# The remainder's low-part passes of two outputs of each first-layer weight pair as two 64-row matmuls in two halves of the TensorE array

## The chip, the core and the metric

The kernel is one program on one core of a Trainium2 chip. The metric is the device time of one execution in microseconds (us), median of several runs. The core has a matrix engine (TensorE, PE in the profile, with its weight loads listed apart as PEld), a vector engine (DVE), a scalar engine (ACT), GpSimd (POOL) and a queue that issues the transfers (SP). They run side by side and wait for each other through semaphores.

## What is computed

The input x has 2048 tokens of width 576. It is normalised per token, and a sum of three terms is returned: x itself, a local attention on the normalised x, and a two-layer network with the mish activation on it:

```python
def _B_ref(x, w1, b1, w2):
    h = jnp.einsum("bsd,df->bsf", x, w1) + b1          # 576 -> 4608
    sp = jnp.log1p(jnp.exp(-jnp.abs(h))) + jnp.where(h > 0, h, jnp.zeros_like(h))
    act = h * jnp.tanh(sp)
    return jnp.einsum("bsf,fd->bsd", act, w2)           # 4608 -> 576

x = A_x
xn = _layernorm(x, axis=-1)
return x + _A_ref(xn, A_wqkv, A_wo) + _B_ref(xn, B_w1, B_b1, B_w2)
```

The change is in the first layer of that network, x times w1.

## The kernel before

**Numbers in two parts.** A float32 operand is split into a high part (a cast to the matmul's own format) and a low part (what the cast dropped). A product is then three matmuls: high by high, low by high, high by low. `prod` (L652) issues these three for two blocks of 128 contraction rows, six matmuls of 128x512.

**The contraction of 576** is four blocks of 128 rows and a remainder of 64. The remainder is not run as 64 rows: the last 64 rows of every weight are there twice, one copy below the other, so a remainder weight has 128 rows. On the x side the 128 rows hold the high part in one half and the low part in the other. One matmul with the high weights then gives high by high and low by high at once. A second one, with the low weights, adds high by low; only the half with the high part of x matters there, and the other half adds low by low, which is far below the precision that is kept. `rest` (L661) issues the two: `wl` 0 with the high weights, `wl` 1 with the low ones. The second is the half-filled pass of the title.

**The x tiles.** A half `hf` of the tokens has two blocks `b` of 512 tokens. `XTs[hf, b]` (tile `xt`) holds x transposed: slots 0 to 3 the high blocks, slot 4 the remainder, 5 to 8 the low blocks. For b = 1 a slot 9 holds the remainder of the difference of the two token blocks. `transpose_split` (L68) fills it, once for each 128 tokens: five or six transposes on PE, a copy to the high slots on ACT, a subtraction for the low slots on DVE. For the remainder the ACT copy writes all 128 rows, and the DVE subtraction (L89) replaces rows 64 to 127 by the low part, for slot 4 and, where it exists, slot 9 in one instruction.

**The first layer** runs over 18 pairs `q` of 128-column weight blocks for each half `hf`, 36 in all. With a Strassen-like scheme of seven products a pair gives four outputs (two token blocks by two weight blocks). `m1_part` (L715) issues it in six parts. Banks of PSUM accumulate: `cur[1]` (tile `h1`), `cur[2]` (`h2`), `cur[3]` (`h3`). Snapshots of `cur[1]` are copied out by ACT in `take` (L691: c11, c21, c22), and `mish` (L694) adds a bank to a snapshot on DVE (L702), applies the activation on ACT (L703) and, in the first half, splits the result. Parts 0, 3, 4 and 5 each end with a `rest`: on `cur[2]`, `cur[1]`, `cur[3]` and `cur[1]`. Parts 4 and 5 are the two that the change touches: part 4 finishes `cur[3]` with the weight `wa` and slot 4, part 5 finishes `cur[1]` with the weight `wc` and slot 9.

**The order** is written out by hand. `quad` puts the parts of a pair in a plan, between chunks of the second layer (`m2_pair` L747, `p_item`, `m2_cols` L858: 24 matmuls of 128x288 each). In 34 of the 36 pairs part 4 comes ahead of part 5, with a chunk of the second layer between them in nearly all of them; in the first pair of each half part 5 comes ahead. Attention (POOL products, DVE sums), weight splitting and transfers are placed by the same plan, so that each engine has one fixed sequence.

Of the kernel before, what the change touches and what calls it, by code (L numbers as in the profile page):

```python
# [8 lines left out]
F32 = mybir.dt.float32  # L9
# [8 lines left out]
P = 128  # L18
# [21 lines left out]
def block_kernel(ctx: ExitStack, tc: tile.TileContext, x, wq, wo, w1, b1, w2, mask, out):  # L40
    nc = tc.nc
# [27 lines left out]
    def transpose_split(src, dst, col, extra=None, pair=False):  # L69
        n = next(tpn)  # L70
        if pair:
            ta, tb = (ps.tile([P, 512], F32, tag="out", bufs=4, name=f"tt{k}_{n}") for k in range(2))
        else:
            ta = ps.tile([P, 512], F32, tag="h", bufs=4, name=f"ta_{n}")
            tb = ps.tile([P, 512], F32, tag="h", bufs=4, name=f"tb_{n}")
        for k in range(KT):
            nc.tensor.transpose(ta[:, k * P:(k + 1) * P], src[:, k * P:(k + 1) * P], ident)
        nc.tensor.transpose(tb[:, 0:P], src[:, KT * P:(KT + 1) * P], ident)
        if extra is not None:
            nc.tensor.transpose(tb[:, P:2 * P], extra, ident)  # L80
        tav = ta.rearrange("p (k t) -> p k t", k=KT)
        hi = dst[:, 0:KT, col:col + P]
        nc.scalar.copy(hi, tav)  # L83
        nc.vector.tensor_sub(dst[:, 5:5 + KT, col:col + P], tav, hi.bitcast(F32))
        e = 1 if extra is None else 2
        hr = dst[:, KT:KT + 5 * e - 4:5, col:col + P]
        tbv = tb.rearrange("p (k t) -> p k t", k=KT)[:, 0:e]
        nc.scalar.copy(hr, tbv)
        nc.vector.tensor_sub(hr[64:P], tbv[64:P], hr[64:P].bitcast(F32))  # L89

    XTs = {}
    rems = {}
# [93 lines left out]
    def ln_transpose(hf, b, jj):  # L186
        if jj == 0:
            XTs[hf, b] = sb.tile([P, 9 + b, TB], F32R, tag=f"xt{b}", bufs=1, name=f"xt_{hf}_{b}")
        xn = xns[hf, b * JB + jj]
        if (b, jj) == (0, 0):  # L190
            rems[hf] = sb.tile([P, JB, P], F32, tag="tt", bufs=2, name=f"rem_{hf}")
        rem = rems[hf][:, jj, :]
        if b == 0:
            nc.gpsimd.tensor_copy(rem, xn[:, KT * P:])
        else:
            nc.gpsimd.tensor_tensor(out=rem, in0=rem, in1=xn[:, KT * P:], op=ALU.subtract)
        transpose_split(xn, XTs[hf, b], jj * P, rem if b else None, (hf, b) == (1, 0) and jj < 3)
# [449 lines left out]
    cur = {}  # L647
    late = []

    def bank(hf, q, n):  # L650
        cur[n] = ps.tile([P, TB], F32, tag="h", bufs=4, name=f"h{n}_{hf}_{q}")
        return cur[n]  # L652

    def prod(ph, wt, off, X, hi, lo, first, last):
        seq = [(off + k, wl, xs + k) for k in range(2) for wl, xs in ((0, hi), (0, lo), (1, hi))]
        for i, (wk, wl, xs) in enumerate(seq):
            nc.tensor.matmul(ph, wt[:, wl, wk * P:(wk + 1) * P], X[:, xs, :],  # L657
                             start=first and i == 0, stop=last and i == len(seq) - 1,
                             skip_group_check=True)

    def rest(ph, wt, off, X, xs):  # L661
        for wl in range(2):
            nc.tensor.matmul(ph, wt[:, wl, off * P:(off + 1) * P], X[:, xs, :], start=False, stop=wl == 1,  # L663
                             skip_group_check=True)

    seven = lambda hf, q: hf == 1 and q <= 2 * OC
# [19 lines left out]
    def take(hf, q, name):  # L686
        if seven(hf, q):
            t = cur[name] = raw_act(q, *dict(c11=(0, 0), c21=(1, 0), c22=(1, 1))[name])
        else:
            t = cur[name] = sb.tile([P, TB], F32, tag="mn", bufs=5, name=f"{name}_{hf}_{q}")  # L690
        nc.scalar.copy(t, cur[1])  # L691

    def mish(hf, q, b, j, ph, t=None):
        f = 2 * (Q1[q] if hf else q) + j  # L694
        n = f"{hf}_{b}_{f}"
        fresh = t is None
        if fresh:
            t = raw_act(q, b, j) if seven(hf, q) else sb.tile([P, TB], F32, tag="mn", bufs=5, name=f"mn_{n}")

        def run():  # L700
            if not fresh:
                nc.vector.tensor_tensor(out=t, in0=ph, in1=t, op=ALU.add)  # L702
            nc.scalar.activation(t, ph if fresh else t, AF.Mish, bias=b1c[:, f:f + 1])  # L703
            if seven(hf, q):
                held_[q, f"A{b + 1}{j + 1}"] = f"A{b + 1}{j + 1}"
                return
            a = acts[hf, q, b, j] = sb.tile([P, 2, TB], F32R, tag=f"a{b}", bufs=(3, 2)[b], name=f"act_{n}")
            nc.scalar.copy(a[:, 0, :], t)  # L708
            nc.gpsimd.tensor_tensor(out=a[:, 1, :], in0=t, in1=a[:, 0, :].bitcast(F32), op=ALU.subtract)  # L709
        if q or b != j:  # L710
            pend.append(run)
        else:
            late.append(run)

    def m1_part(hf, q, part):  # L715
        X0, X1 = XTs[hf, 0], XTs[hf, 1]
        if part == 5 and late:
            for fn in late[::-1]:
                fn()
            late.clear()  # L720
        wa, wc, t0, t1 = (done.get((k, hf, q)) for k in ("wa", "wc", "t0", "t1"))
        if part == 0:
            prod(bank(hf, q, 1), wa, 0, X0, 0, 5, True, True)
            take(hf, q, "c11")
            prod(bank(hf, q, 2), wa, 2, X0, 2, 7, True, False)
            rest(cur[2], wa, 4, X0, 4)
            mish(hf, q, 0, 0, cur[2], cur["c11"])
        elif part == 1:
            prod(bank(hf, q, 3), t1, 0, X1, 0, 5, True, True)
        elif part == 2:  # L730
            prod(cur[1], t0, 2, Ss[hf, 1], 0, 2, False, True)
            take(hf, q, "c21")
        elif part == 3:
            prod(cur[1], t0, 0, Ss[hf, 0], 0, 2, False, False)
            rest(cur[1], wc, 2, X1, 4)
            take(hf, q, "c22")
        elif part == 4:
            prod(cur[3], t1, 2, X1, 2, 7, False, False)
            rest(cur[3], wa, 4, X1, 4)
            mish(hf, q, 1, 0, cur[3], cur["c21"])  # L740
        else:
            prod(cur[1], wc, 0, Ss[hf, 2], 0, 2, False, False)
            rest(cur[1], wc, 2, X1, 9)
            mish(hf, q, 0, 1, cur[1])
        if part == 3:
            mish(hf, q, 1, 1, cur[3], cur["c22"])
# [406 lines left out]
    def mi(hf, q, part, alias=None):  # L1153
        add(("m", hf, q, part), lambda: m1_part(hf, q, part), alias=alias)
# [178 lines left out]
    def spot(hf, q, i):  # L1333
        return at["s", hf, q, i]
# [97 lines left out]
    for n in range(8):  # L1432
        c, k = divmod(n, 4)
# [57 lines left out]
    k = marks[0] - 1  # L1491
    for n in range(2 * steps):
        t = n * total / (2 * steps)
        if n == steps:
            k = max(k, spot(1, 0, 0) + 1)
        k = next(k for k in range(k + 1, len(plan)) if T[k + 1] > t and ok[k])
# [11 lines left out]
    for n, name in enumerate(("T3", "T1", "T2", "T4", "B11", "B21", "B22", "R", "D")):  # L1508
        k = i + 10 + (0,5,10,15,20,25,30,35,40)[n]
# [74 lines left out]
```

## Time and profile before

| what | before |
|---|---|
| median of 3 runs | 1124.03 us (1123.45 to 1124.14) |
| span of the profiled execution, first to last instruction | 1121.6 us |
| PE busy | 1109.5 us, 99% of the span |
| PE weight loads busy | 1023.0 us, 91% |
| DVE, ACT, POOL busy | 829.0, 492.1, 787.7 us |
| granted PE clock | 1.000 over the span |

No time is listed for the profiled execution apart from its span; the median of the runs is 2.4 us above that span. A line of the page's groups reads: line of the kernel, engine, operation, output from inputs, count, then busy time, mean duration of one in ns, and the engine's idle time ahead of the group with what ended it. A line of the timeline reads: start, length, engine, line, operation, operands, count. PE's records overlap: a 128x512 matmul's record is some 390 ns long while the next one starts some 227 ns after it, so the rate is read from starts, not from durations.

### The profile page before, as it was taken

What the parts mean: (1) busy time and instruction counts of PE and PEld (TensorE: products, weight loads), DVE (VectorE), ACT (ScalarE), POOL (GpSimd) and SP (SyncE); (2) the same over time, 40 slices, a digit from 0 to 9 for tenths busy, and PEclk for the clock granted to TensorE, in tenths of its full rate; (3) what the DMA queues carried; (4) which work ended last, traced back from release to release, by engine and by line L of the source; (5) the groups of instructions that cost most, each with busy time, mean ns of one, the idle gap of its engine ahead of it and who ended that gap; (6) DMA issues with size and microseconds to landing.
All of it is one profiled execution on the core that took longest, in us unless ns stands there. A gap on an engine that the chain in (4) does not pass through costs nothing.

```text
span 1121.6 us, 18415 instructions
## 1 busy us (share of the span) xinstructions
PE 1109.5 (99%) x6630; PEld 1023.0 (91%) x6630; DVE 829.0 (74%) x1351; ACT 492.1 (44%) x892; POOL 787.7 (70%) x639
## 2 busy tenths in 40 slices
PE   8999999999999999999999999999999999999998
PEld 7999899999999999899999889999999999999998
DVE  6368788888888888877655456687866677776876
ACT  5544645544554545455233355343433343443332
POOL 2488767767689687676788476665789878668632
PEclk9999999999999999999999999999999999999999
DMA  6899885868767849666596797655655477676463
GB/s 200 283 312 318 290 283 205 289 228 284 261 240 258 282 163 345 222 240 214 191 342 238 231 373 249 241 200 174 227 198 189 168 263 269 215 253 248 157 222 104
DMA packets 147487, 271.08 MB, mean 242 GB/s; under 512 B 30114, under 2 KB 86724, under 8 KB 147396
## 3 DMA queue, kind: packets, MB, share of 16 engines
q1 hardware_dynamic: 147396, 269.91, 69.2%
q8 instruction: 52, 0.85, 0.3%
q14 instruction: 39, 0.32, 0.1%
HBM read 160.39 MB, written 109.48 MB: 241 GB/s over the span
## 4 chain that ended last, share of the span: by engine, by line
PE 89%; DVE 4%; POOL 3%; DMA 2%; issue 1%; ACT 1%; DVEq 0%; POOLq 0%; SPq 0%
PE h L657 28%; PE po L755 19%; PE pq L349 11%; PE po L868 10%; PE po L847 7%; PE h L663 5%; PE o L1056 4%; PE z L447 2%; DMA acc<-in_x 1%; POOL accP L856 1%; DVE u L801 1%; POOL pr L534 0%; DVE accP L871 0%; POOL act L709 0%; DMA z_B<-kept_wq 0%
## 5 line engine op out<-in xcount | busy, mean ns | idle before, releaser
L755 PEld LDWEIGHTS po<-w,act 128*128 128x128 f32 x1728 | 236.4, 188 | 7.5 <-DVE acc L759 1.7
L755 PE MATMUL po<-w,act 128*128 128x288 f32 x1728 | 240.8, 295 | 1.4 <-DVE acc L759 1.2
L534 POOL TENSOR_TENSOR pr<-q,kv 128x576 f32<-128x576 f32 x128 | 195.7, 1553 | 18.7 <-DMA q<-q_d 16.9
L572 POOL TENSOR_TENSOR pv<-L,kv 128x576 f32<-128x576 f32 x128 | 174.3, 1461 | 38.7 <-DVE L L565 20.9
L709 POOL TENSOR_TENSOR act<-c,act 128x512 fp32r<-128x512 f32 x81 | 107.1, 1322 | 128.4 <-ACT act L708 125.5
L759 DVE TENSOR_TENSOR acc<-po,acc 128x288 f32<-128x288 f32 x288 | 120.4, 450 | 31.6 <-PE po L755 30.2
L349 PE MATMUL pq<-wq,xt 128*128 128x432 f32 x672 | 136.2, 361 | 1.8 <-ACT xt L83 1.8
L868 PEld LDWEIGHTS po<-w,act 128*128 128x128 f32 x960 | 131.1, 188 | 3.7 <-DVE accP L871 0.4
L868 PE MATMUL po<-w,act 128*128 128x288 f32 x960 | 133.8, 295 | 0.2
L349 PEld LDWEIGHTS pq<-wq,xt 128*128 128x128 f32 x672 | 125.0, 188 | 8.7 <-ACT xt L83 2.7
L703 ACT ACTIVATE c<-c,b1c 128x512 f32<-128x512 f32 x81 | 58.7, 724 | 132.9 <-DVE c L702 132.6
L657 PE MATMUL h<-xt,t 128*128 128x512 f32 x432 | 110.6, 391 | 0.9 <-DVE c L702 0.8
L657 PE MATMUL h<-S,t 128*128 128x512 f32 x432 | 110.4, 391 | 0.0
L691 ACT COPY c<-h 128x512 f32<-128x512 f32 x81 | 47.4, 586 | 136.5 <-PE h L663 78.3
L578 DVE TENSOR_REDUCE og<-pv 128x144 f32<-128x1152 f32 x64 | 85.9, 1343 | 25.4 <-POOL pv L572 25.4
L657 PE MATMUL h<-xt,wa 128*128 128x512 f32 x432 | 104.0, 390 | 0.0
L657 PEld LDWEIGHTS h<-xt,wa 128*128 128x128 f32 x432 | 80.9, 188 | 16.9
L871 DVE TENSOR_TENSOR accP<-po,accP 128x288 f32<-128x288 f32 x160 | 69.6, 454 | 36.1 <-PE po L868 34.5
L847 PEld LDWEIGHTS po<-pw,u 128*128 128x128 f32 x672 | 92.4, 188 | 2.9 <-DVE u L801 0.5
L847 PE MATMUL po<-pw,u 128*128 128x288 f32 x672 | 94.2, 296 | 0.3 <-DVE u L801 0.3
L539 DVE TENSOR_REDUCE L<-pr 128x64 f32<-128x1152 f32 x64 | 85.8, 1341 | 11.2 <-POOL pr L534 11.1
L657 PEld LDWEIGHTS h<-xt,t 128*128 128x128 f32 x432 | 79.0, 188 | 16.1 <-DVE c L702 1.1
(231 smaller groups left out, 1840.5 us busy)
## 6 DMA issues: line engine op xcount, KB each, us to landing
kv<-kv_d SPq DMA_DIRECT2D x64, 396.0 KB, 5.2
kept_t<-t SPq DMA_DIRECT2D x36, 512.0 KB, 5.3
t<-kept_t SPq DMA_DIRECT2D x36, 512.0 KB, 5.4
rw<-in_w SPq DMA_DIRECT2D x36, 320.0 KB, 4.6
kept_wa<-wa SPq DMA_DIRECT2D x18, 640.0 KB, 3.5
kept_w<-w SPq DMA_DIRECT2D x20, 576.0 KB, 4.8
wa<-kept_wa SPq DMA_DIRECT2D x18, 640.0 KB, 6.1
w<-kept_w SPq DMA_DIRECT2D x20, 576.0 KB, 4.5
```

What stands on the lines that cost most here:

```text
L349: nc.tensor.matmul(pq[:, 0:432], XT[:, xi, tok], wt[wi][:, hl, 0:432], start=i == 0, stop=i == len(seq) - 1)
L534: nc.gpsimd.tensor_tensor(out=pr[:, x:x + hh], in0=q[:, j0 + x:j0 + x + hh, None, :].to_broadcast([P, hh, W, CU]), in1=win(kt, 0, CU, j0 + ...
L539: nc.vector.tensor_reduce(L[:, k, j0:j0 + hj].rearrange("p j w h -> p (j w h)"), pr.rearrange("p j w (h d) -> p (j w h) d", h=2), axis=AX, ...
L572: nc.gpsimd.tensor_tensor(out=pr[:, x:x + hj].rearrange("p j d w -> p j w d"), in0=L[:, k, x:x + hj, :, h:h + 1].to_broadcast([P, hj, W, DH]),
L578: nc.vector.tensor_reduce(og[:, :, c0:c0 + DH], pr, axis=AX, op=ALU.add)
L657: nc.tensor.matmul(ph, wt[:, wl, wk * P:(wk + 1) * P], X[:, xs, :], start=first and i == 0, stop=last and i == len(seq) - 1, skip_group_ch ...
L709: nc.gpsimd.tensor_tensor(out=a[:, 1, :], in0=t, in1=a[:, 0, :].bitcast(F32), op=ALU.subtract)
L755: nc.tensor.matmul(po, acts[hf, q, b, j][:, al, tok], done["w2", hf, 2 * q + j][:, wl, c * HC:(c + 1) * HC], start=i == 0, stop=i == 5)
L759: nc.vector.tensor_tensor(out=t, in0=po, in1=t, op=ALU.add)
L847: nc.tensor.matmul(po, units[e, k, qq][:, al, tok], w[:, qq, wl, :], start=i == 0, stop=i == 5)
L868: nc.tensor.matmul(po, acts[hf, q, b, j][:, al, tok], done["w2", hf, 2 * q + j][:, wl, c * HC:(c + 1) * HC], start=i == 0, stop=i == 5)
L871: nc.vector.tensor_tensor(out=t, in0=po, in1=t, op=ALU.add)
```

## The change

Of the four half-filled passes of a pair, those of parts 4 and 5 go. `rest` gets a switch `high` that leaves the low-weight matmul out, and a new function `rest_low` issues both outputs' low-weight products as two matmuls of 64 rows each, one behind the other: for `cur[3]` rows 64 to 127 of `wa` and slot 4, for `cur[1]` rows 0 to 63 of `wc` and slot 9. They are called once for a pair, at the end of whichever of parts 4 and 5 comes first. So that rows 64 to 127 of slot 4 hold the high part in the b = 1 tiles, `transpose_split` puts the low part into rows 0 to 63 of slot 4 there and into rows 64 to 127 of slot 9, with two DVE instructions in place of one. The two remainder passes of parts 0 and 3 stay as they were.

```diff
         nc.scalar.copy(hr, tbv)
-        nc.vector.tensor_sub(hr[64:P], tbv[64:P], hr[64:P].bitcast(F32))
+        if extra is None:
+            nc.vector.tensor_sub(hr[64:P], tbv[64:P], hr[64:P].bitcast(F32))
+        else:
+            for r, k in ((slice(0, 64), 0), (slice(64, P), 1)):
+                nc.vector.tensor_sub(hr[r, k], tbv[r, k], hr[r, k].bitcast(F32))
...
-    def rest(ph, wt, off, X, xs):
-        for wl in range(2):
+    def rest(ph, wt, off, X, xs, high=False):
+        for wl in range(1 if high else 2):
             nc.tensor.matmul(ph, wt[:, wl, off * P:(off + 1) * P], X[:, xs, :], start=False, stop=wl == 1,
                              skip_group_check=True)
+
+    def rest_low(wa, wc, X1):
+        for ph, wt, off, xs, r in ((cur[3], wa, 4, 4, slice(64, P)), (cur[1], wc, 2, 9, slice(0, 64))):
+            nc.tensor.matmul(ph, wt[r, 1, off * P:(off + 1) * P], X1[r, xs, :], start=False, stop=True,
+                             skip_group_check=True)
...
         elif part == 4:
             prod(cur[3], t1, 2, X1, 2, 7, False, False)
-            rest(cur[3], wa, 4, X1, 4)
+            rest(cur[3], wa, 4, X1, 4, True)
+            if cur.pop("lows", None) is None:
+                rest_low(wa, wc, X1)
+                cur["lows"] = True
             mish(hf, q, 1, 0, cur[3], cur["c21"])
         else:
             prod(cur[1], wc, 0, Ss[hf, 2], 0, 2, False, False)
-            rest(cur[1], wc, 2, X1, 9)
+            rest(cur[1], wc, 2, X1, 9, True)
+            if cur.pop("lows", None) is None:
+                rest_low(wa, wc, X1)
+                cur["lows"] = True
             mish(hf, q, 0, 1, cur[1])
```

On PE the order shows the following at the end of part 4 of pair 6 in the first half (`hf` 0), before: six matmuls of `prod`, two of `rest`, then the second layer's chunk.

```order
L657 MATMUL h3_0_6_2828<-xt_0_1_515,t1_0_6_2708 128x512 [waits DVE_49]
L657 MATMUL h3_0_6_2828<-xt_0_1_515,t1_0_6_2708 128x512 x5
L663 MATMUL h3_0_6_2828<-xt_0_1_515,wa_0_6_2537 128x512 x2
```

After the change, at the same place (lines have moved by 4; L672 is in `rest_low`):

```order
L661 MATMUL h3_0_6_2832<-xt_0_1_515,t1_0_6_2712 128x512 [waits DVE_49]
L661 MATMUL h3_0_6_2832<-xt_0_1_515,t1_0_6_2712 128x512 x5
L667 MATMUL h3_0_6_2832<-xt_0_1_515,wa_0_6_2541 128x512
L672 MATMUL h3_0_6_2832<-xt_0_1_515,wa_0_6_2541 128x512
L672 MATMUL h1_0_6_2804<-xt_0_1_515,wc_0_6_2610 128x512 [waits Activation_49]
```

One full matmul has become one 64-row matmul on the same bank, and behind it stands the other output's 64-row matmul on bank `h1`, which now carries a wait for ACT (the copy c22 out of that bank). Part 5 of the same pair on PE before:

```order
L657 MATMUL h1_0_6_2800<-S2_0_800,wc_0_6_2606 128x512 [waits Activation_49]
L657 MATMUL h1_0_6_2800<-S2_0_800,wc_0_6_2606 128x512 x5
L663 MATMUL h1_0_6_2800<-xt_0_1_515,wc_0_6_2606 128x512 x2
```

And after:

```order
L661 MATMUL h1_0_6_2804<-S2_0_804,wc_0_6_2610 128x512 x6
L667 MATMUL h1_0_6_2804<-xt_0_1_515,wc_0_6_2610 128x512
```

Part 5 has lost its last matmul, and its wait for ACT has moved ahead to the 64-row matmul in part 4. The order of the other engines is unchanged but for eight DVE instructions of 64x2x128 (four for each half) that are now sixteen of 64x128.

## The prediction

> **What bounds the kernel now.** I read the page's busy shares first, then the chain that ended last, then who waited for whom.
>
> ```profile
> span 1121.6 us, 18415 instructions
> PE 1109.5 (99%) x6630; PEld 1023.0 (91%) x6630; DVE 829.0 (74%) x1351; ACT 492.1 (44%) x892; POOL 787.7 (70%) x639
> PEclk9999999999999999999999999999999999999999
> PE 89%; DVE 4%; POOL 3%; DMA 2%; issue 1%; ACT 1%; DVEq 0%; POOLq 0%; SPq 0%
> PE h L657 28%; PE po L755 19%; PE pq L349 11%; PE po L868 10%; PE po L847 7%; PE h L663 5%; PE o L1056 4%; PE z L447 2%; DMA acc<-in_x 1%; POOL accP L856 1%; DVE u L801 1%; POOL pr L534 0%; DVE accP L871 0%; POOL act L709 0%; DMA z_B<-kept_wq 0%
> ```
>
> PE is busy throughout at its full clock, and 89% of the chain is PE. A busy PE could still hide waits, so the list of PE's own waits decides. These are its longest, and the list holds little more:
>
> ```profile
> PE pq L349 <- ACT xt L83: 1.8, 2, 1.1
> PE o L1056 <- DVE y L1060: 1.3, 2, 0.7
> PE h L657 <- DVE c L702: 0.8, 1, 0.8
> PE h L657 <- ACT rt L691: 0.7, 1, 0.7
> ```
>
> PE hardly ever waits. So a microsecond taken out of PE's sequence inside the first layer is a microsecond off the end, and one added there is one on the end. The other engines have a quarter of the span or more to spare and follow.
>
> **What is removed.** The passes concerned are in these two groups (line, operation, count, then busy time, mean ns, idle time):
>
> ```profile
> L663 PE MATMUL h<-xt,wc 128*128 128x512 f32 x144 | 45.0, 394 | 0.0
> L663 PE MATMUL h<-xt,wa 128*128 128x512 f32 x144 | 44.4, 389 | 0.0
> ```
>
> 288 remainder passes are 8 for each of 36 pairs; the change takes 2 of the 8, so 72 go, and 72 matmuls of 64 rows come. The duration of 390 ns is no price, since the records overlap. The price is the distance between starts, read in the timeline of PE in one part 4:
>
> ```profile
> 302.39 1.53 PE L657 MATMUL h<-xt,t 128*128 128x512 f32 x6
> 303.76 0.61 PE L663 MATMUL h<-xt,wa 128*128 128x512 f32 x2
> 304.21 0.29 PE L755 MATMUL po<-w,act 128*128 128x288 f32 x1
> ```
>
> From 302.39 to 304.21 stand eight matmuls: 1.82 / 8 = 0.227 us each. Removed are 72 x 0.227 = 16.4 us of PE time, 0.454 us for a pair.
>
> **What is added** is 36 times two 64-row matmuls of 512 columns on different rows of the array and different banks. No row of this trace shows a matmul of 64 rows: all groups of PE read 128*128. So its price has to be bounded.
>
> If the two halves run fully at once, two take the time of one, and a pair gains 0.227 us: 36 x 0.227 = 8.2 us. That is the lower end. How late the second starts behind the first depends on its weights. The weight loads of the same stretch:
>
> ```profile
> 302.26 1.24 PEld L657 LDWEIGHTS h<-xt,t 128*128 128x128 f32 x6
> 303.53 0.41 PEld L663 LDWEIGHTS h<-xt,wa 128*128 128x128 f32 x2
> 303.99 0.41 PEld L755 LDWEIGHTS po<-w,act 128*128 128x128 f32 x2
> ```
>
> The load for the matmul at 303.76 starts at 303.53, which is when the matmul before it starts (302.39 + 5 x 0.227 = 303.53). The next load starts one pitch later, with the matmul at 303.76. So in the steady stream each load goes out when the matmul ahead of it starts, one at a time. Applied here: the first half's weights load under the last full matmul and cost nothing; the second half's weights go out when the first half's matmul starts. How long a load then holds its matmul back shows where matmuls are short, in the transposes of 128 columns:
>
> ```profile
> 41.70 0.56 PE L349 MATMUL pq<-wq,xt 128*128 128x432 f32 x2
> 42.09 0.60 PE L77 MATMUL ta<-ident,xn 128*128 128x128 f32 x4
> 42.52 0.27 PE L78 MATMUL tb<-ident,xn 128*128 128x128 f32 x1
> 42.63 0.27 PE L80 MATMUL tb<-ident,rem 128*128 128x128 f32 x1
> 42.66 0.84 PE L349 MATMUL pq<-wq,xt 128*128 128x432 f32 x3
> ```
>
> Four of them start within 0.43 us (42.09 to 42.52): 0.108 us for one load and one short matmul. I take 0.108 us as the lag of the second half, because it is the nearest row on load against load. A pair then costs 0.227 + 0.108 = 0.335 us in place of 0.454, and gains 0.119 us: **36 x 0.119 = 4.3 us**.
>
> The Trainium skill, "TensorE: Matmul & The Clock Gate", section "Part 3: Packing small matmuls — row/col tiling", says that matmuls on different row groups start about 4 ns apart, since the loads of other row groups are pulled ahead. With its 4 ns the sum would be an estimated 8.0 us. No run here shows it; the same section's remark that loads overlap running matmuls only on other row groups is not what this trace has, where full loads start as full matmuls start.
>
> The larger unknown is what it costs to go from 128-row work to 64-row work and back, 72 switches in all. The nearest change of kind in this trace is the rows above, where transposes follow ordinary matmuls and are followed by them. From 42.09 to 42.66 there is 0.57 us for six transposes, under 6 x 0.108 = 0.65, and the matmul behind them merely has a long record (three take 0.84). The switch itself shows no gap. From the other side, a switch could cost what it costs to let the array run empty and start again: the record's 0.389 less the pitch of 0.227, 0.162 us of tail, and the weights loaded in the open. This row shows a restart after a wait:
>
> ```profile
> 636.10 1.66 PE L657 MATMUL h<-S,wc 128*128 128x512 f32 x6 [0.68 <-ACT rt L691]
> ```
>
> Six matmuls take 1.66 where the stream above takes 1.53, so the open load is 0.13 us. A switch then costs between nothing and 0.162 + 0.13 = 0.29 us. I take nothing, as at the transposes, and keep 0.29 for the range: 72 x 0.29 = 20.9 us against the gain of 4.3 is 16.6 us slower.
>
> **The moved wait.** The second half's matmul waits for ACT's copy c22 out of bank `h1`, where before part 5's first matmul did. Behind it on PE stands everything, so a late copy would stop the whole kernel. The timeline of PE and ACT at the end of a part 3 of the first half, one part ahead of the part 4 shown above; under it DVE's two additions at the part 5 that comes first in its half:
>
> ```profile
> 298.76 0.61 PE L663 MATMUL h<-xt,wc 128*128 128x512 f32 x2
> 299.41 0.59 ACT L691 COPY c<-h 128x512 f32<-128x512 f32 x1 [0.42 <-PE h L663]
> ...
> 636.08 0.69 DVE L702 TENSOR_TENSOR rt<-h,rt 128x512 f32<-128x512 f32 x1 [6.43 <-ACT rt L691]
> 636.68 0.68 DVE L702 TENSOR_TENSOR ra<-h,ra 128x512 f32<-128x512 f32 x1
> ```
>
> The copy is done at 300.00, and the new place of the wait is where the second L663 matmul stands, 303.76 + 0.227 = 303.99. Four microseconds of second-layer work cover it. In the two pairs with part 5 first the new wait is for DVE's addition out of `h3`, one of the two shown. Both are done by 637.36, and part 5, begun at 636.10, reaches the new place after seven matmuls, at 637.69. I cost the wait at nothing. If a copy slipped by more than the cover, its excess would be added for that pair.
>
> **DVE's eight more instructions** for the x tiles:
>
> ```profile
> L89 DVE TENSOR_TENSOR xt<-tb,xt 64x256 fp32r<-64x256 f32 x8 | 3.4, 429 | 0.2
> L89 DVE TENSOR_TENSOR xt<-tb,xt 64x128 fp32r<-64x128 f32 x5 | 1.5, 295 | 0.2
> ```
>
> Eight of 429 ns become sixteen of 295 ns: 16 x 0.295 - 8 x 0.429 = 1.3 us more on DVE. Nothing on PE waited for L89, and the b = 1 tiles are wanted only behind other projections, so they cost nothing; without that cover 1.3 us in all. Transfers and the queues of SP and POOL do not change.
>
> **The sum.** 1121.6 - 4.3 = 1117.3 us of span; the median lies 2.4 us above the span, so **1119.7 us**.
>
> **The rivals.**
>
> *The switch drains the array.* The full-width results in flight must leave before half-width work may start, and the other way round, at the end of part 4 (part 5 in two pairs). [...] Against it: the transposes show no gap. With the tail at both switches a pair costs 0.335 + 2 x 0.162 = 0.659 against 0.454, 36 x 0.205 = 7.4 us more: 1131.4 us. It decides from 0.119 / 2 = 0.06 us a switch; with the open load as well it is 1140.6. The Trainium skill, "TensorEngine Tiling (Array Packing)", section "Key Properties", states that changing the tiling mode drains the TensorE. By that rule this rival wins if the drain is over 0.06 us; no run here shows it, since no tile here is narrow.
>
> *The halves do not overlap.* If the second matmul waits for the first, say because the moving rows or the bank writes are shared, two 64-row matmuls cost 0.454 us as two full ones did, and nothing changes: 1124.0. A drain near 0.06 us lands here too. For it speaks that nothing in this trace ever runs two matmuls at once; against it, that the operands and banks are disjoint.
>
> *Everything overlaps*, both loads pulled ahead: 8.2 us, 1115.8.
>
> **How the numbers follow.** Free switches with a lag of about one load: 0.35. Everything overlaps: 0.12. No net change: 0.20. Drain: 0.33, of which about a third above 1132. The range reaches from the full overlap, 1115.5, to 1132, a little beyond the drain with hidden loads, and leaves out some 0.13. About 0.2% (2.2 us) is what a measurement of this kernel can tell from no change. The two overlapping cases are faster (0.47), the next same (0.20), the drain slower (0.33).
>
> **What would show it.** In the changed profile the 64-row rows should stand as 64*128 on L672, 72 of them. Right: the starts of the two are about 0.11 us apart, the first comes 0.227 after the full matmul, and the next full matmul 0.227 after the second. Wrong by drain: a gap of more than 0.227 ahead of the first, or more than that between the second and the next full one, and PE's weight loads pausing there. Wrong by no overlap: the two 0.227 apart. The forecast would also fail if PE's waits on L672 grew, which the list of waits would name with ACT behind it.

## The result, and the profile after

| what | before | after |
|---|---|---|
| median | 1124.09 us (1123.45 to 1124.54, 4 runs) | 1131.06 us (1130.74 to 1131.52, 4 runs) |
| span of the profiled execution | 1121.6 us | 1129.7 us |
| ratio, 95% interval | | 1.0062 (1.005 to 1.0074) |

The change makes the kernel 0.6% slower, some 7 us. The two spans lie further apart, 8.1 us, because each is that of a single execution: in every run that lists both, the time is some 1.8 us above the span, so the profile before is of an execution near the lowest of its four times and the profile after of the one with the highest. The lines of the page that answer to those shown before:

```profile
span 1129.7 us, 18430 instructions
PE 1115.9 (99%) x6630; PEld 1013.4 (90%) x6630; DVE 828.6 (73%) x1359; ACT 492.0 (44%) x892; POOL 789.0 (70%) x639
PE 90%; DVE 4%; DMA 2%; issue 2%; POOL 1%; ACT 1%; DVEq 0%; SPq 0%; POOLq 0%
```

PE issues as many matmuls as before and is still the bound, at a granted clock of 1.0. Its weight loads are *less* busy, 1013.4 us against 1023.0, and "issue", time in which an engine waited for nothing that the profile shows, has gone from 1% to 2% of the chain. The view of the new line's instructions (count, shortest, median and longest duration in ns, then what its engine had been idle for) says where:

```profile
L672 PEld LDWEIGHTS h<-xt,wa x36: 182/183/183, 112.7 to 1040.4; 64*128 64x128 f32 x36
L672 PE MATMUL h<-xt,wa x36: 491/492/499, 112.7 to 1040.4; 64*128 64x512 f32 x36
L672 PEld LDWEIGHTS h<-xt,wc x36: 182/183/184, 112.7 to 1040.4; 64*128 64x128 f32 x36
L672 PE MATMUL h<-xt,wc x36: 490/491/494, 112.7 to 1040.4; 64*128 64x512 f32 x36
  issue: 12.4, 35
  DVE c L711: 0.4, 1
```

The 72 matmuls are there as 64*128. The last two lines are about the weight loads: ahead of the first of each two they paused 35 times for 12.4 us in all, 0.35 us each, with nothing to wait for that the profile shows. The 36th pause, of 0.4 us, is put down to an addition on DVE. Next the timeline of PE (start, length, engine, line, operands, count) over one part 4, a chunk of the second layer and a part 5, after:

```profile
303.56 1.53 PE L661 MATMUL h<-xt,t 128*128 128x512 f32 x6
304.94 0.39 PE L667 MATMUL h<-xt,wa 128*128 128x512 f32 x1
305.25 0.49 PE L672 MATMUL h<-xt,wa 64*128 64x512 f32 x1
305.26 0.49 PE L672 MATMUL h<-xt,wc 64*128 64x512 f32 x1
305.68 3.46 PE L770 MATMUL po<-w,act 128*128 128x288 f32 x24
308.97 1.53 PE L661 MATMUL h<-S,wc 128*128 128x512 f32 x6
310.34 0.39 PE L667 MATMUL h<-xt,wc 128*128 128x512 f32 x1
310.57 1.75 PE L661 MATMUL h<-xt,wa 128*128 128x512 f32 x7
```

The weight loads around the two halves, at the same place after:

```profile
304.71 0.19 PEld L667 LDWEIGHTS h<-xt,wa 128*128 128x128 f32 x1
305.25 0.18 PEld L672 LDWEIGHTS h<-xt,wa 64*128 64x128 f32 x1 [0.35 <-issue]
305.25 0.18 PEld L672 LDWEIGHTS h<-xt,wc 64*128 64x128 f32 x1
305.68 3.22 PEld L770 LDWEIGHTS po<-w,act 128*128 128x128 f32 x24 [0.24 <-issue]
```

The matmuls before, from the chunk on:

```profile
304.21 3.34 PE L755 MATMUL po<-w,act 128*128 128x288 f32 x24
307.39 1.53 PE L657 MATMUL h<-S,wc 128*128 128x512 f32 x6
308.76 0.61 PE L663 MATMUL h<-xt,wc 128*128 128x512 f32 x2
309.21 2.88 PE L657 MATMUL h<-xt,wa 128*128 128x512 f32 x12
```

Read the starts. The two halves begin within 0.01 us of each other, so they do run side by side. But the first begins 0.31 us behind the last full matmul (304.94 to 305.25), where the stream's distance is 0.227: 0.09 us too late. The next full matmul begins 0.42 us behind the second half, where 0.227 would be the stream. And the chunk behind it takes 3.46 us instead of 3.34: its second matmul, and all behind it, is another 0.12 us late. The loads say why. The load of the last full matmul started at 304.71, with the matmul ahead of it (303.56 + 5 x 0.227 = 304.70), and was hidden. The halves' loads start at 305.25 and the chunk's first load at 305.68, each only when its own matmul is listed to start, so they are in the open. In all, from the start of part 4 to the end of part 5, it was 302.39 to 309.21 = 6.82 us and is 303.56 to 310.57 = 7.01. A pair lost 0.19 us where 0.119 was to be gained. 36 x 0.19 = 6.8 us, with rows rounded to 0.01 us some 6 to 7.5.

What the spans differ by beyond that stands in the list of PE's waits. New in it, or longer:

```profile
PE po L883 <- DVE accP L886: 1.2, 2, 1.0
PE h L661 <- DVE rt L711: 0.7, 1, 0.7
PE z L451 <- DVE zqs L464: 0.5, 1, 0.5
```

They are a few places in the second half of the kernel. No wait on L672 is in PE's list, so the moved wait cost nothing.

### The profile page after: what moved, and what is told of

The parts are those of the page before. It is cut to its first block, busy times and chain, and to the rows that moved or that the text cites. A ratio compares the mean times of both kernels' runs of the same rounds, so it can differ in the third digit from the quotient of the medians.

```text
span 1129.7 us, 18430 instructions
## 1 busy us (share of the span) xinstructions
PE 1115.9 (99%) x6630; PEld 1013.4 (90%) x6630; DVE 828.6 (73%) x1359; ACT 492.0 (44%) x892; POOL 789.0 (70%) x639
## 4 chain that ended last, share of the span: by engine, by line
PE 90%; DVE 4%; DMA 2%; issue 2%; POOL 1%; ACT 1%; DVEq 0%; SPq 0%; POOLq 0%
PE h L661 29%; PE po L770 19%; PE pq L353 11%; PE po L883 10%; PE po L862 8%; PE o L1071 4%; PE h L667 4%; PE z L451 2%; PE h L672 1%; DMA acc<-in_x 1%; DVE accP L886 1%; DMA z_B<-kept_wq 1%; POOL pr L538 0%; DVE L L543 0%; PE ta L77 0%
## 5 line engine op out<-in xcount | busy, mean ns | idle before, releaser
L538 POOL TENSOR_TENSOR pr<-q,kv 128x576 f32<-128x576 f32 x128 | 195.8, 1555 | 18.2 <-DMA q<-q_d 16.4
```

The source lines that it names most:

```text
L538: nc.gpsimd.tensor_tensor(out=pr[:, x:x + hh], in0=q[:, j0 + x:j0 + x + hh, None, :].to_broadcast([P, hh, W, CU]), in1=win(kt, 0, CU, j0 + ...
```

## The experiments

The theory after this reading, called **S** in the expectations: the cost is the switch between full and half width. On the way in, PE waits until the array has emptied, and the halves' weights then load in the open. (That the 0.09 us are the array running empty is a reading of the gap. The trace shows the gap and the late load.) On the way out the same happens to the next full matmul. The rival **C**: the two halves disturb each other side by side. A third, **L**: the new layout of the x tiles delays something. A "visit" is one stay at half width. Unless an edit below says otherwise it is made on the changed kernel.

**The halves apart**: part 4 calls for the half of `cur[3]` alone, part 5 for the half of `cur[1]`.

```diff
-    def rest_low(wa, wc, X1):
-        for ph, wt, off, xs, r in ((cur[3], wa, 4, 4, slice(64, P)), (cur[1], wc, 2, 9, slice(0, 64))):
+    def rest_low(n, wa, wc, X1):
+        for ph, wt, off, xs, r in ((cur[3], wa, 4, 4, slice(64, P)), (cur[1], wc, 2, 9, slice(0, 64)))[n:n + 1]:
...
-            if cur.pop("lows", None) is None:
-                rest_low(wa, wc, X1)
-                cur["lows"] = True
+            rest_low(0, wa, wc, X1)
...
-            if cur.pop("lows", None) is None:
-                rest_low(wa, wc, X1)
-                cur["lows"] = True
+            rest_low(1, wa, wc, X1)
```

> Each 64-row matmul stands alone, at the end of its own part: 72 visits to half width in place of 36. Theory S (the cost is the switch: the array runs empty and the next weights load in the open, once on the way in and once on the way out; the halves themselves overlap fully): in the trace of the change one visit costs 0.62 us of PE time (0.318 + 0.003 + 0.421 - 0.227 and 0.109 on the second matmul behind), a lone half as much as two, so 36 x 0.62 = 22 us over the change: about 1153 us. Theory C (the two halves contend for a port when side by side, the switch is cheap): apart they don't contend, so each costs a full pass at most and the time falls to 1124 or below.

Measured: 1151.42 us, ratio 1.0247 (1.0232 to 1.0262). C is out: with no neighbour to disturb them, twice as many visits cost 20.4 us more than the change, where S expected 22.

**One half only**

```diff
-        for ph, wt, off, xs, r in ((cur[3], wa, 4, 4, slice(64, P)), (cur[1], wc, 2, 9, slice(0, 64))):
+        for ph, wt, off, xs, r in ((cur[3], wa, 4, 4, slice(64, P)),):
```

> Only the half of the first output is issued; the low-weight product of the second output is left out. Theory S: a visit costs the same with one half as with two, since the second starts 3 ns behind the first: 1131 us, within 1.5. Theory C: without its neighbour the half runs freely, and 36 x 0.1 to 0.2 us go: 1124 to 1127 us.

Measured: 1130.46 us, ratio 1.0058 (1.0043 to 1.0073). That is 0.6 us under the change for all 36 visits, and the two intervals overlap: the second half of a visit costs next to nothing. The timeline of this kernel:

```profile
304.64 0.39 PE L667 MATMUL h<-xt,wa 128*128 128x512 f32 x1
304.96 0.49 PE L672 MATMUL h<-xt,wa 64*128 64x512 f32 x1
305.38 0.80 PE L770 MATMUL po<-w,act 128*128 128x288 f32 x4
```

The distances are those of the change, 0.32 and 0.42 us, for one half alone.

**The pair of halves twice in one visit**

```diff
-        for ph, wt, off, xs, r in ((cur[3], wa, 4, 4, slice(64, P)), (cur[1], wc, 2, 9, slice(0, 64))):
+        for ph, wt, off, xs, r in ((cur[3], wa, 4, 4, slice(64, P)), (cur[1], wc, 2, 9, slice(0, 64))) * 2:
```

> The pair of halves is issued twice in a row, so the low products of both outputs are added twice. Theory S: no switch between them, the second pair costs one stream of 512 columns, 0.227 us: 36 x 0.227 = 8.2 over the change, 1139 us. Theory C (a pair side by side costs 0.42 us in itself, as the distance to the next matmul shows): 36 x 0.42 = 15 over it, 1146 us.

Measured: 1138.11 us, ratio 1.0127 (1.011 to 1.0144). The second pair of halves cost 7.05 / 36 = 0.20 us, about one stream of 512 columns and well under the 0.42. (The trace below has it at 0.33 + 0.32 - 0.42 = 0.23; this run's list of PE's waits sums to 1.3 us less than that of the change.) Its timeline takes the switch apart:

```profile
306.49 0.39 PE L667 MATMUL h<-xt,wa 128*128 128x512 f32 x1
306.81 0.50 PE L672 MATMUL h<-xt,wa 64*128 64x512 f32 x1
306.81 0.50 PE L672 MATMUL h<-xt,wc 64*128 64x512 f32 x1
307.14 0.39 PE L672 MATMUL h<-xt,wa 64*128 64x512 f32 x1
307.15 0.39 PE L672 MATMUL h<-xt,wc 64*128 64x512 f32 x1
307.47 3.46 PE L770 MATMUL po<-w,act 128*128 128x288 f32 x24
```

And its weight loads there:

```profile
306.80 0.18 PEld L672 LDWEIGHTS h<-xt,wa 64*128 64x128 f32 x1 [0.35 <-issue]
306.91 0.19 PEld L672 LDWEIGHTS h<-xt,wa 64*128 64x128 f32 x1
307.47 0.82 PEld L770 LDWEIGHTS po<-w,act 128*128 128x128 f32 x6 [0.37 <-issue]
```

The first halves' records are 0.50 us long, the second halves' 0.39: the difference of 0.11 is a weight load in the open, and it shows as 306.81 to 307.14 = 0.33 = 0.227 + 0.10. Loads of 64 rows are not always in the open: the second one for `wa` starts at 306.91, while the first matmul on the same rows still runs, and is hidden. Only the loads that follow a change of width, those at 306.80 and 307.47, start with their own matmul. From the second halves to the full matmul there are 0.32 us, 0.227 and 0.09 of emptying, as on the way in. Then the chunk takes 3.46 instead of 3.34, the next open load. So a switch costs about 0.09 + 0.11 = 0.20 us, a visit two of them, 0.40 (with the halves' own stream of 0.227 that is the 0.62 of the expectations). What the two halves gain in a visit is one full pass, 0.227. The difference, 0.17, is the loss.

**Both low-weight products left out**, by the same edit in parts 4 and 5:

```diff
             if cur.pop("lows", None) is None:
-                rest_low(wa, wc, X1)
+                pass
                 cur["lows"] = True
```

> Both low-weight products of parts 4 and 5 are left out. Both theories: PE sets the end, so the 36 visits of 0.62 us go from the change, 1131 - 22 = 1109, and the same from before: 1124 - 72 x 0.227 = 1108. A time well above 1110 would say that another engine or a wait takes over.

Measured: 1110.79 us, ratio 0.9886 (0.9871 to 0.99). 20.3 us of the change are its visits, 0.56 us each, and a little under the 0.62 of the trace, because PE's waits grow where its work is taken out: their list sums to 12.6 us, that of the change to 10.2. The largest:

```profile
PE po L770 <- DVE acc L774: 2.0, 2, 1.7
PE po L883 <- DVE accP L886: 1.9, 2, 1.6
```

**The x layout alone**, in the kernel before:

```diff
-        nc.vector.tensor_sub(hr[64:P], tbv[64:P], hr[64:P].bitcast(F32))
+        if extra is None:
+            nc.vector.tensor_sub(hr[64:P], tbv[64:P], hr[64:P].bitcast(F32))
+        else:
+            for r, k in ((slice(0, 64), 0), (slice(64, P), 1)):
+                nc.vector.tensor_sub(hr[r, k], tbv[r, k], hr[r, k].bitcast(F32))
```

> The kernel before with one part of the change alone: the two DVE subtractions for the x tiles in place of one. Theory S: hidden, 1124 us within 0.7. Theory L (the changed layout work delays the x tiles, and PE's other waits in the changed trace come from it): up to 1.3 us more, or as much as the 7 us of the change.

Measured: 1124.13 us, ratio 1.0 (0.9991 to 1.0009). The DVE work is hidden; L is out.

**Both halves on the same rows**

```diff
-        for ph, wt, off, xs, r in ((cur[3], wa, 4, 4, slice(64, P)), (cur[1], wc, 2, 9, slice(0, 64))):
+        for ph, wt, off, xs, r in ((cur[3], wa, 4, 4, slice(64, P)), (cur[1], wc, 2, 9, slice(64, P))):
```

> The second half uses the same rows of the array as the first (rows 64 to 127), where slot 9 holds the low part, so the second output gets low by low in place of its low-weight product. Theory S: on the same rows nothing overlaps, the second starts one stream later: 36 x 0.22 = 8 us over the change, 1139 us. If the overlap did not depend on the rows: 1131 us.

Measured: 1138.72 us, ratio 1.013 (1.0116 to 1.0143), 7.7 us over the change. Side by side is a matter of the rows, and the rival that the halves do not overlap is out: where they don't, the kernel comes to this time and not to that of the change. In this kernel's timeline the second half starts 0.34 us behind the first:

```profile
306.53 0.50 PE L672 MATMUL h<-xt,wa 64*128 64x512 f32 x1
306.87 0.39 PE L672 MATMUL h<-xt,wc 64*128 64x512 f32 x1
307.19 1.06 PE L770 MATMUL po<-w,act 128*128 128x288 f32 x6
```

**96 rows**, in the kernel before, with `low96` set for part 5's call:

```diff
-            nc.tensor.matmul(ph, wt[:, wl, off * P:(off + 1) * P], X[:, xs, :], start=False, stop=wl == 1,
+            r = slice(0, 96) if wl and low96 else slice(0, P)
+            nc.tensor.matmul(ph, wt[r, wl, off * P:(off + 1) * P], X[r, xs, :], start=False, stop=wl == 1,
```

> The kernel before, with the low-weight pass of part 5 cut from 128 rows to 96, alone in its place; 36 such matmuls. If the switch is due to the number of row groups that differs from the stream's, it costs what the lone half cost, 0.39 us a visit above a full pass: 36 x 0.39 = 14 us over before, 1138 us. If it is due to the array being divided in halves, which 96 rows don't ask for, nothing changes: 1124 us.

Measured: 1124.6 us, ratio 1.0003 (0.9993 to 1.0012). The groups of this kernel have them as 96 rows, and as long as a full one:

```profile
L664 PE MATMUL h<-xt,wc 128*128 128x512 f32 x108 | 36.8, 395 | 0.0
L664 PE MATMUL h<-xt,wc 96*128 96x512 f32 x36 | 14.2, 396 | 0.0
```

Fewer rows than 128 are no switch in themselves; 64 are.

**Four halves in one visit**: the doubled visit of above, and the half-filled passes of parts 0 and 3 taken out too.

```diff
-            rest(cur[2], wa, 4, X0, 4)
+            rest(cur[2], wa, 4, X0, 4, True)
...
-            rest(cur[1], wc, 2, X1, 4)
+            rest(cur[1], wc, 2, X1, 4, True)
```

> All four half-filled passes of a pair are taken out as full ones and four 64-row matmuls stand in one visit, two in each half. The visits' products go to the two banks that are open there, so two outputs lack theirs and two have theirs twice; it is the price that is asked for. Theory S: one visit of 0.62 us plus one more stream of 0.227 in place of four full passes of 0.227: 36 x (0.85 - 0.91) = 2 us under before, 1122 us, within 1.5. Theory C: 0.62 + 0.42 in place of 0.91, 1129 us.

Measured: 1125.77 us, ratio 1.0014 (1.0005 to 1.0023): a miss by 3.8 us. The timeline's distances of a visit are those of the doubled one, which is 0.05 us less than four full passes, some 1.9 us in all. But PE's waits have grown, and eat more than that:

```profile
PE po L883 <- DVE accP L886: 1.5, 2, 1.2
PE h L661 <- DVE c L711: 1.1, 1, 1.1
PE h L661 <- DVE rt L711: 1.1, 1, 1.1
PE z L451 <- DVE zqs L464: 0.6, 1, 0.6
```

Added up, the whole list, of which these are four rows, has 11.0 us, 2.7 over the list of before. That leaves about 0.9 us of the 3.6 between the count and the measurement without an account. The waits for `rt` and `zqs` are also in the 96-row kernel, which has no visit, with 0.9 and 0.5 us. So they come and go when the order is shifted a little; what sets them was not settled.

**The visit ahead of its part's matmuls**: the call of `rest_low` moved above `prod` in parts 4 and 5, and the mark of the last matmul of a sum (`stop`) moved with it.

> The visit stands at the start of its part, ahead of the six matmuls of prod and mostly behind second-layer matmuls of 288 columns; all products are there. Theory S with a fixed tail: the wait ahead of the halves is 0.09 us over the 288-column pitch of 0.133, as it was over the 512-column pitch of 0.227, the visit costs the same and the time is that of the change, 1131 us within 1.5. If the wait grows with the length of the matmul ahead, it is about 0.05 us here, and 36 x 0.04 = 1.5 us less: 1129.5.

Measured: 1129.81 us, ratio 1.0052 (1.0035 to 1.0069), between the two expectations. The timeline decides:

```profile
302.31 0.96 PE L770 MATMUL po<-w,act 128*128 128x288 f32 x6
303.20 0.49 PE L672 MATMUL h<-xt,wa 64*128 64x512 f32 x1
303.20 0.50 PE L672 MATMUL h<-xt,wc 64*128 64x512 f32 x1
303.63 1.65 PE L661 MATMUL h<-xt,t 128*128 128x512 f32 x6
```

The sixth 288-column matmul starts at 302.31 + 5 x 0.133 = 302.98, the halves 0.22 behind it: 0.09 us over the pitch, as behind 512 columns. The wait ahead of the halves does not grow with the matmul ahead. The six matmuls behind take 1.65 instead of 1.53, the open load again. The 1.2 us less than the change are not in the visit: this run's list of PE's waits sums to 8.7 us, that of the change to 10.2.

**One pass for both**, in the kernel before, with the switch `high` of the change added to `rest`:

```diff
-            rest(cur[1], wc, 2, X1, 9)
+            rest(cur[1], wc, 2, X1, 9, True)
```

> The kernel before without the second output's half-filled pass in part 5; its low-weight product is left out and nothing comes in its place, as if the pair of halves had cost one pass and no switch. PE sets the end: 36 x 0.227 = 8.2 us under before, 1116 us; up to 2 us more if waits take over as they did with both passes left out (1110.8 where 1108 follows from the count).

Measured: 1116.6 us, ratio 0.9933 (0.9918 to 0.9948). That is about what the change would have given if the switch were free and the halves fully side by side. No version that computes all products came out faster than the kernel before. One that gathers four half-filled passes of the right banks in a visit would need another order of the parts, and wasn't tried.

## Why the prediction was wrong, point by point

- **PE is the bound, work taken out of it comes off the end.** Right: 36 passes less gave 7.5 us for 8.2, 72 gave 13.2 for 16.4, the rest of the 72 going into longer waits. The list of PE's waits held more than the prediction said: three rows of 0.9 to 1.3 us (`warm`, `po` on L755, `ta`) stand in it beside the four that are shown, 8.3 us in all.
- **Price of a full pass, 0.227 us from starts.** Right.
- **Lag of the second half, 0.108 us.** Wrong: it is within 0.01 us, and one half alone costs the same. Its weights don't wait for the first half's matmul to start: both loads start at 305.25. The first half's weights were to load under the last full matmul "and cost nothing". That failed too: their load starts 0.31 us behind that matmul's start and costs 0.11. Here the Trainium skill's 4 ns ("TensorE: Matmul & The Clock Gate", "Part 3: Packing small matmuls — row/col tiling") agrees with the trace's 0.01 us or less.
- **The switch is free, "as at the transposes".** Wrong, and this is the step that failed. The transposes use all rows of the array as their neighbours do; they show that this change of operation is free (six in 0.57 us) and say nothing of a change of width, just as the 96-row matmuls show nothing. Measured were a gap of 0.09 us and 0.11 us of open weight load at each of 72 switches, 0.20 against the 0.06 from which the prediction saw the loss begin, or 0.11 with no lag between the halves. The Trainium skill's rule that a change of tiling mode drains the array ("TensorEngine Tiling (Array Packing)", "Key Properties") fits the 0.09 us; the trace has no row that shows the array empty.
- **The drain as a rival**, with its chance of 0.33 and 1131.4 us, was the case that came. That it hit 1131.06 so closely is luck, since its errors cancel: the emptying was taken as 0.162 from the records' length and the gap is 0.09, the lag was taken as 0.108 and is nothing, and the open load of 0.11 at each switch was left out of it. So it has 2 x 0.162 + 0.108 = 0.43 us for a visit where 2 x 0.20 = 0.40 were measured. The 0.20 of a switch lies within the bounds of nothing and 0.29 that the prediction gave it.
- **The other two rivals.** "Everything overlaps" was right about the two halves and wrong about the switches. "The halves do not overlap" is wrong about the halves: on the same rows, where they follow one another, the kernel is 7.7 us slower still.
- **The moved wait and DVE's instructions cost nothing.** Right: no wait of PE on L672, and 1124.13 us with the layout alone.
- Of the 8.1 us between the two spans, 6 to 7 are the visits. PE's waits, 8.3 us in all in the list of before and 10.2 in that of after, are the rest; how much of these 1.9 us belongs to the change and how much to the single execution profiled was not settled.

## What to carry to other kernels

Two 64-row matmuls side by side save one full pass of 512 columns (0.227 us) but pay for a visit to half width twice 0.20 us. In a stream of full-width matmuls like this one, a visit therefore pays only where it saves more than 0.40 us, nearly two full passes. Gather half-width work into long runs, or leave it as half-filled full-width passes. When a price has no row in the trace, ask what property the nearest row shares with the unknown: here it had to be the division of the array, and the transposes did not share it.

## What was not expected of the hardware

- The weights of both halves load together: both are listed at 305.25 us in the stretch shown for the change, and the second costs next to nothing (1130.46 us with one half, 1131.06 with two), while full loads in the stream go out one at a time, one for each matmul.
- A load behind a change of width starts with its own matmul, 0.31 us after the start of a 512-column matmul ahead of it. Behind no change of width, a 64-row load starts 0.11 us after the load ahead of it, on the same rows and under a running matmul (306.80 and 306.91 us in the doubled visit).
- A lone 64-row matmul of 512 columns takes PE out of its stream for 0.62 us (0.32 + 0.42 - 0.227 and 0.11 on the matmul behind), nearly three full passes; a 96-row one costs no more than a full pass (ratio 1.0003).
- The gap at a switch is 0.09 us over the usual distance whether the matmul ahead has 288 or 512 columns.
- A PE stream with more work taken out gains less: 13.2 of 16.4 us with 72 passes gone, with DVE's additions out of PSUM as the new waits.
